# Filler products moved ahead of a gather's transposes, and one routing step fewer ahead of the first expert

## The chip, the cores and the metric

The kernel runs on one core of a Trainium2 chip. The metric is the device time of one execution in microseconds (us): 960.69 before the change, the median of three runs (960.13 to 963.97).

## The reference

Three layers follow each other: a local and global attention, a dense gated layer, and a mixture of 8 experts with balanced routing. The change lies in the last one, which computes this (N = 2304 tokens, D = 512, E = 8 experts, F = 1024):

```python
def _moe2_ref(x, w_gate, w1, w2):
    cap = N // E
    logits = x @ w_gate
    order = np.argsort(-logits.flatten())
    for idx in order:
        tok, e = idx // E, idx % E
        if assigned[tok] >= 0 or counts[e] >= cap:
            continue
        assigned[tok] = e
        counts[e] += 1
    for e in range(E):
        mask = assigned == e
        h = np.maximum(x[mask] @ w1[e], 0.0)
        out[mask] = h @ w2[e]
```

In the kernel there are 17 groups of 128 tokens and each expert takes 272 tokens. The expert that fills first is fixed first, its tokens leave the others' lists, and so on: eight routings, one after the other, each giving the number of an expert and its list of tokens.

## The kernel before, in words

Up to about 652 us the kernel computes attention and the dense layer; the change leaves that alone. Then come eight routings (`route(j)`) and eight experts (`ffn(j)`), and the next routings are woven into the experts.

**A routing.** Each token's best remaining expert is written as a bitmap in bfloat16 (`oh8`, two copies on ScalarE, L929, 2 us together). Then six **counts** search for the threshold, digit by digit: VectorE compares (`ge`, L910 or L948), TensorE counts with 17 products `rt<-ge,oh` (L961), VectorE reads the number and forms the next comparison. After the sixth count the expert's number `ei` is known (L982); SyncE (SP) reads it (L983), and only then can the loads of that expert's weights start. The list of tokens follows: two products with the selected tokens (L1001, L1002), positions on VectorE (L1004 to L1018), 17 products with `obi` (L1022), three with `zs` (L1028), the indices, and three indirect DMAs on GpSimd (POOL) that **gather** the tokens' rows, 128, 128 and 16 of them (`gather`, L1059).

**An expert.** `x_pair(j)` turns the gathered rows with TensorE's transposes (L1101, into the PSUM tile `T`, two buffers) and splits them into a high part `xh` (ScalarE) and a remainder `xl` (VectorE). Weights come as 8 loads of 512 KB (`er`, four buffers, SP, L1071), split the same way: the **cast** `eh` on ScalarE (L1080) and the **remainder** `el` on POOL (L1083). The gate phase makes 8 tiles of 12 products (L1136) in the PSUM tile `A` (three buffers), each read by ScalarE (`fh`) and VectorE (`fl`); the down phase makes 4 tiles of 24 products (L1152). `y_rows(j)` turns the result back (L1115) and scatters it.

**The order.** A scheduler orders each engine's instructions by dependencies and a model; the program narrows this. `visit` notes an instruction of the routing, `behind` orders the next product of an expert after it (and only that one): the routing goes first. `step_route` runs the routing to its next `yield`, and the number yielded says how many parts of the running expert may pass before the next step. `warm(n)` (L879 to L886) makes n **unread products** of 128x512 into an `A` tile, whose result nobody reads; there are three behind each count of routing 0, two behind the first two counts of routing 1, and twenty behind routing 0's last products, in the time in which the first tokens are gathered. At the end of the program's set-up stand `x_pair(0)` and three `step_route()`, then the loop over experts.

Of the kernel before, what the change touches and what calls it, by code (L numbers as in the profile page):

```python
# [24 lines left out]
NT = NTOK // 128  # L25
# [8 lines left out]
def body(ctx, tc, units, gk, gv, wts, w2g, w1, w2, cst, cst2, out):  # L34
    nc = tc.nc
    gp, sy = nc.gpsimd, nc.sync
    NS, SY = (mybir.DependencyInfo(c, mybir.DependencyReason.DATA)
              for c in (mybir.DependencyClass.NoSync, mybir.DependencyClass.Sync))
# [19 lines left out]
    ve, sc, te = nc.vector, nc.scalar, nc.tensor  # L58
# [4 lines left out]
    ident = consts.tile([128, 128], F32, name="ident")  # L63
# [801 lines left out]
    def small(shape, name, dt=F32, bufs=2):  # L865
        return rt.tile(shape, dt, name=name, bufs=bufs)
# [3 lines left out]
    VISIT = []  # L870

    def behind(ins):

        if VISIT:
            tc.add_manual_dep(ins.ins, VISIT.pop().ins.name, NS, reason="routing first")

    def visit(ins):
        VISIT[:] = [ins]

    def warm(n):  # L880

        for _ in range(n):
            pw = p2.tile([128, 512], F32, name="A", bufs=3)
            q = te.matmul(pw, tri, mask.rearrange("p v w -> p (v w)")[:, :512], start=True, stop=True)
            behind(q)
            visit(q)  # L886

    def route(j):

        first = j == 0  # L890
        m = small([128, NT], "m0", bufs=1) if first else M[j % 2]
        S = small([128, 2, NT], "S", BF16)
        if j < NE - 1:
# [3 lines left out]
            oh8 = small([128, NT, 16, NE], "oh8", BF16, bufs=1)  # L897
# [5 lines left out]
            d = small([128, NT], "d0", bufs=1) if first else dplace()  # L903
            lo = small([128, NT], "lo")
            ge = small([128, NT, 64], "ge", BF16, bufs=2)
# [8 lines left out]
            for a, z in ((0, NT - 1), (NT - 1, NT)) if first else ((0, NT),):  # L914
                n = z - a
# [8 lines left out]
                for c0, c1 in cuts:  # L924
# [3 lines left out]
                    else:  # L928
                        q = sc.activation(oh8[:, c0:c1], src, AF.Copy)  # L929
# [11 lines left out]
            for r, th in enumerate((kt0, kt1, kt2, kt3, kt1, kt2)):  # L941
                K = 32 if r % 3 else 64
                if r:
                    ge = small([128, NT, 64], "ge", BF16, bufs=2)
                    for c0, c1 in ((0, 9), (9, NT)):
                        n = c1 - c0
                        tb, db = th[:, None, :].to_broadcast([128, n, K]), d[:, c0:c1, None].to_broadcast([128, n, K])
                        ve.scalar_tensor_tensor(ge[:, c0:c1, :K], tb, nn, db, op0=OP.add, op1=OP.is_le)  # L948
                    e = dplace()
                    ve.tensor_scalar(e, d, nn, 64.0 if r == 3 else 32.0, op0=OP.subtract, op1=OP.mult)  # L950
                    if r % 3 == 2:
                        ve.tensor_scalar(e, e, 1057.0, None, op0=OP.add)
                        if r == 2:
                            ve.tensor_tensor(e, e, lo, op=OP.add)
                    d = e
                if first and r == 0:
                    fill_bank(FIRST_GE[0])
                yield 2 if r == 3 or j == 1 else 3
                pc = p2.tile([128, 512], F32, name="rt", bufs=1)
                for c in range(NT):  # L960
                    visit(te.matmul(pc[:, :K], oh8[:, c].rearrange("p a e -> p (a e)"), ge[:, c, :K],  # L961
                                    start=(c == 0), stop=(c == NT - 1)))
                if j == 0:
                    warm(3)
                elif j == 1 and r < 2:
                    warm(2)
                ok = small([128, 64], "ok", BF16)
                ne = small([128, 1], "ne")
                ve.tensor_scalar(ok[:, :K], pc[:, :K], float(CAP), None, op0=OP.is_ge, op1=OP.add, accum_out=ne)
                nn = small([128, 1], "nn")  # L970
                ve.tensor_reduce(nn, ne.to_broadcast([128, 32]), axis=AX.X, op=OP.max, apply_transpose=True)
# [44 lines left out]
        ve.tensor_tensor(oa, ab[:, 0, :, None].to_broadcast([128, NT, 17]),  # L1016
                         i17[:, None, :].to_broadcast([128, NT, 17]), op=OP.is_equal)
        ve.tensor_tensor(obi, ob, ids_b[:, :, None].to_broadcast([128, NT, 16]), op=OP.mult)  # L1018
        yield 3 if j == 1 else 4
        pz = p2.tile([128, 512], F32, name="rt", bufs=1)  # L1020
        for c in range(NT):
            visit(te.matmul(pz[:17, :16], oa[:, c], obi[:, c], start=(c == 0), stop=(c == NT - 1)))  # L1022
# [5 lines left out]
            visit(te.matmul(pi[:, 16 * g:16 * g + 16], spread[:, g], zs, start=True, stop=True))  # L1028
        if j == 0:
            warm(20)  # L1030
        it = small([128, 3, 16], "it")
        ve.tensor_tensor(it, pi[:, :48].rearrange("p (g b) -> p g b", g=3),
                         pick[:, None, :].to_broadcast([128, 3, 16]), op=OP.mult)
# [59 lines left out]
    def x_pair(j):  # L1093

        xg = XG.pop(j)
        xh = fw.tile([128, 4, CAP], F32R, name="xh", bufs=2)
        xl = fw.tile([128, 4, CAP], F32R, name="xl", bufs=2)
        for g, n in GR:
            pt = p2.tile([128, 4, 128], F32, name="T", bufs=2)
            for d in range(4):  # L1100
                te.transpose(pt[:, d, :n], xg[:n, g, 128 * d:128 * d + 128], ident[:n, :n])  # L1101
            o = slice(128 * g, 128 * g + n)
            XH_LAST[:] = [sc.activation(xh[:, :, o], pt[:, :, :n], AF.Copy)]
            ve.tensor_tensor(xl[:, :, o], pt[:, :, :n], xh[:, :, o], op=OP.subtract)
            if g == 2:
                XP[j] = (xh, xl)
            yield
# [100 lines left out]
    step_route()  # L1208
    for _ in x_pair(0):
        pass  # L1210
    for _ in range(3):
        step_route()
    for j in range(NE):
        while j not in ROUTED:
# [110 lines left out]
```

## Time and profile before

| what | us |
|---|---|
| median of 3 runs | 960.69 (960.13 to 963.97) |
| the profiled execution | 965.33 |
| its span (first to last instruction) | 963.6 |
| TensorE busy, share of the span | 871.9, 90% |
| VectorE | 611.1, 63% |
| ScalarE | 453.0, 47% |
| GpSimd | 371.9, 39% |

The mean granted clock of TensorE is 0.951 of full speed. In the chain of work that ended last TensorE has 68%, VectorE 12%, DMA 5%, and 7% is time in which an engine waited for nothing that the profile shows. Busy shares are means over the whole span: what the routings and the experts wait for is read from windows and timelines of the last third. PE is TensorE, DVE VectorE, ACT ScalarE, POOL GpSimd, SP SyncE.

### The profile page before, as it was taken

The numbers are of one execution on the slowest core, as the hardware profiler recorded it, in microseconds if no ns is written. First come the engines' busy times: TensorE is split into PE (matmuls) and PEld (weight loads), VectorE is DVE, ScalarE is ACT, GpSimd is POOL, SyncE is SP. The second block draws the span as 40 slices with busy tenths as digits, with TensorE's granted clock in tenths as the row PEclk, the third lists the DMA queues.
The fourth block names the chain that finished last, engine by engine and source line by source line (L and its number), as shares of the span: only waits on it lengthen the run. The fifth ranks groups of instructions, "written<-read, shape, count | busy, mean of one in ns | idle before, by whom it ended". The sixth has DMA issues, their size and how long they took to land.

```text
span 963.6 us, 19509 instructions
## 1 busy us (share of the span) xinstructions
PE 871.9 (90%) x7556; PEld 732.3 (76%) x7556; DVE 611.1 (63%) x1859; ACT 453.0 (47%) x923; POOL 371.9 (39%) x344
## 2 busy tenths in 40 slices
PE   5677699999999999989979989996789989999996
PEld 4566578777788887778758757783488988999996
DVE  3677699999328579597595484268666766763210
ACT  4656454555247465445354333230554364545531
POOL 2444333444212222113111111121666786687841
PEclk8889889999999999989989999997789999999998
DMA  9631243542212233303221020001454455446600
GB/s 373 254 121 45 86 155 132 160 161 66 88 66 93 85 103 108 118 29 109 82 78 56 27 74 1 1 23 43 169 184 142 133 185 188 135 149 215 197 28 26
DMA packets 28497, 108.10 MB, mean 112 GB/s; under 512 B 3572, under 2 KB 3572, under 8 KB 28276
## 3 DMA queue, kind: packets, MB, share of 16 engines
q1 hardware_dynamic: 25332, 97.94, 30.0%
q0 software_dynamic: 3072, 8.92, 2.6%
q8 instruction: 59, 0.97, 0.4%
q14 instruction: 34, 0.28, 0.1%
HBM read 97.92 MB, written 8.91 MB: 111 GB/s over the span
## 4 chain that ended last, share of the span: by engine, by line
PE 68%; DVE 12%; issue 7%; DMA 5%; POOL 4%; ACT 3%; SPq 0%; POOLq 0%; ACTq 0%; DVEq 0%
PE G L564 26%; PE X L588 11%; PE A L1152 7%; PE A L1136 5%; PE rt L961 2%; DMA er<-w 2%; DMA xg<-xs,idx 2%; DVE junk L523 2%; DVE ge L948 1%; POOL wp L50 1%; PE PV L476 1%; PE PV L399 1%; POOL vl L50 1%; PE T L1101 1%; DMA gkr<-gv 1%
## 5 line engine op out<-in xcount | busy, mean ns | idle before, releaser
L564 PEld LDWEIGHTS <-wp 128*128 128x128 f16 x2592 | 231.6, 99 | 80.5 <-issue 52.0
L564 PE MATMUL G<-xth,wp 128*128 128x256 f16 (+1 forms) x1344 | 235.8, 270 | 4.1 <-ACT xth L434 2.5
L578 POOL TENSOR_TENSOR hl<-th,hh 128x256 fp32r<-128x256 f32 (+1 forms) x108 | 85.5, 792 | 348.1 <-ACT hh L576 274.8
L564 PE MATMUL G<-xtl,wp 128*128 128x256 f16 (+1 forms) x672 | 177.5, 270 | 4.3 <-DVE xtl L435 4.3
L1083 POOL TENSOR_TENSOR el<-er,eh 128x1024 fp32r<-128x1024 f32 x62 | 146.3, 2390 | 40.7 <-ACT eh L1080 40.4
L569 ACT ACTIVATE th<-G,ib 128x256 f32<-128x256 f32 (+1 forms) x108 | 49.4, 459 | 107.8 <-PE G L564 97.0
L571 DVE SCALAR_TENSOR_TENSOR th<-th,G 128x256 f32<-128x256 f32 (+1 forms) x108 | 43.4, 402 | 81.9 <-ACT th L569 81.0
L1080 ACT ACTIVATE eh<-er 128x1024 fp32r<-128x1024 f32 x64 | 65.5, 1054 | 49.4 <-DMA er<-w 43.2
L576 ACT ACTIVATE hh<-th 128x256 fp32r<-128x256 f32 (+1 forms) x108 | 43.4, 402 | 75.4 <-DVE th L573 75.1
L1136 PE MATMUL A<-xh,eh 128*128 128x272 f32 x256 | 77.9, 304 | 0.0
L1152 PE MATMUL A<-fh,eh 128*128 128x272 f32 x256 | 76.6, 302 | 0.0
L1136 PE MATMUL A<-xh,el 128*128 128x272 f32 x256 | 75.2, 294 | 0.0
L1136 PE MATMUL A<-xl,eh 128*128 128x272 f32 x256 | 74.9, 293 | 0.0
L1152 PE MATMUL A<-fh,el 128*128 128x272 f32 x256 | 74.4, 292 | 0.0
L1152 PE MATMUL A<-fl,eh 128*128 128x272 f32 x256 | 74.2, 291 | 0.0
L1141 DVE SCALAR_TENSOR_TENSOR fl<-A,fh 128x272 fp32r<-128x272 f32 x64 | 28.0, 439 | 59.2 <-ACT fh L1140 57.4
L523 DVE SCALAR_TENSOR_TENSOR junk<-xr,w2gt 128x512 f16<-128x512 f32 x80 | 59.0, 737 | 4.1 <-ACT xr L500 3.4
L588 PE MATMUL X<-oh,hh 128*128 128x512 f32 x156 | 57.7, 444 | 2.1 <-ACT hh L576 2.1
L588 PE MATMUL X<-oh,hl 128*128 128x512 f32 x156 | 55.7, 428 | 0.0
L573 DVE SCALAR_TENSOR_TENSOR th<-th,ib,G 128x256 f32<-128x256 f32 (+1 forms) x108 | 50.1, 464 | 2.9
L588 PE MATMUL X<-ol,hh 128*128 128x512 f32 x156 | 51.5, 403 | 0.0
L1136 PEld LDWEIGHTS A<-xl,eh 128*128 128x128 f32 x256 | 49.2, 192 | 0.1
(389 smaller groups left out, 2126.7 us busy)
## 6 DMA issues: line engine op xcount, KB each, us to landing
er<-w SPq DMA_DIRECT2D x64, 512.0 KB, 5.2
wr<-wts SPq DMA_DIRECT2D x36, 512.0 KB, 3.6
unit<-units SPq DMA_DIRECT2D x22, 688.0 KB, 4.0
unit<-gv SPq DMA_DIRECT2D x12, 640.0 KB, 3.8
wp<-units SPq DMA_DIRECT2D x10, 688.0 KB, 7.8
gkr<-gk SPq DMA_DIRECT2D x8, 608.0 KB, 4.7
xs<-xr SPq DMA_DIRECT2D x17, 256.0 KB, 2.0
gkr<-gv SPq DMA_DIRECT2D x4, 640.0 KB, 7.3
```

The lines of the kernel that those rows point to most:

```text
L523: ve.scalar_tensor_tensor(junk[:, :DM], xr, 1.0, w2gt[:, e], op0=OP.mult, op1=OP.mult, accum_out=L[:, c, e:e + 1])
L564: te.matmul(pg[:, j, :n], wp_[:, f, j, a, o], x[:, d, :n], start=(i == 0), stop=(i == 11))
L569: TH[:] = [sc.activation(th[:, :n], pg[:, 0, :n], AF.Tanh, scale=ib[:, 0, f:f + 1])]
L571: ve.scalar_tensor_tensor(t[:, :n], th[:, :n], 1.0, pg[:, 0, :n], op0=OP.add, op1=OP.mult)
L573: mark(ve.scalar_tensor_tensor(h[:, :n], t[:, :n], ib[:, 1, f:f + 1], pg[:, 1, :n], op0=OP.mult, op1=OP.mult))
L576: sc.activation(hh[:, :n], h[:, :n], AF.Copy)
L578: gp.tensor_tensor(hl[:, :n], h[:, :n], hh[:, :n], op=OP.subtract)
L588: te.matmul(self.px[t], a[:, 128 * t:128 * t + 128], w[:, f, :], start=(f == 0 and i == 0), stop=(f == NF - 1 and i == 2))
L1080: q = sc.activation(h, r, AF.Copy)
L1083: q = (ve if j == 0 and i < 2 else gp).tensor_tensor(l, r, h, op=OP.subtract)
L1136: behind(te.matmul(pa_[:, :CAP], a[:, s], x[:, d], start=(i == 0), stop=(i == 11)))
L1152: behind(te.matmul(py[:, :CAP], a[:, s], x[:, f], start=(i == 0), stop=(i == 23)))
```

## The change

Four edits, all in the last layer:

1. The first transpose of `x_pair(0)` is ordered behind the last of the twenty unread products.
2. The first product of routing 1's first count is ordered behind the last transpose of `x_pair(0)`.
3. Two steps instead of three of the next routing in front of the first expert.
4. From routing 2 on the first count comes 5 parts after the step before instead of 3, and the products with `obi` of routing 1 come 4 parts after instead of 3.

```diff
+    WARM, T_LAST = [], []
+
     def visit(ins):
         VISIT[:] = [ins]
+        return ins
...
-                yield 2 if r == 3 or j == 1 else 3
+                yield 2 if r == 3 or j == 1 else 5 if r == 0 and j > 1 else 3
                 pc = p2.tile([128, 512], F32, name="rt", bufs=1)
                 for c in range(NT):
-                    visit(te.matmul(pc[:, :K], oh8[:, c].rearrange("p a e -> p (a e)"), ge[:, c, :K],
-                                    start=(c == 0), stop=(c == NT - 1)))
+                    q = visit(te.matmul(pc[:, :K], oh8[:, c].rearrange("p a e -> p (a e)"), ge[:, c, :K],
+                                          start=(c == 0), stop=(c == NT - 1)))
+                    if j == 1 and r == c == 0:
+                        tc.add_manual_dep(q.ins, T_LAST[0].ins.name, NS, reason="tokens first")
...
-        yield 3 if j == 1 else 4
+        yield 4
         pz = p2.tile([128, 512], F32, name="rt", bufs=1)
...
             warm(20)
+            WARM[:] = VISIT
...
-                te.transpose(pt[:, d, :n], xg[:n, g, 128 * d:128 * d + 128], ident[:n, :n])
+                q = te.transpose(pt[:, d, :n], xg[:n, g, 128 * d:128 * d + 128], ident[:n, :n])
+                T_LAST[:] = [q]
+                if WARM:
+                    tc.add_manual_dep(q.ins, WARM.pop().ins.name, NS, reason="behind the unread products")
...
     for _ in x_pair(0):
         pass
-    for _ in range(3):
+    for _ in range(2):
         step_route()
```

The line numbers of the changed kernel are 3 higher from L879 on and 6 to 9 higher after L1028. All products are the same in number and kind; what moves is their order. Three places show it.

TensorE, between the last of routing 0 and the first count of routing 1, before (`cb` and `mask` are operands of the unread products, `T<-ident,xg` the transposes, `rt<-ge,oh` the count):

```order
L884 MATMUL A<-mask,cb 128x512
L1101 MATMUL T<-ident,xg 128x128 x4
L884 LDWEIGHTS cb
L884 MATMUL A<-mask,cb 128x512
...
L884 MATMUL A<-mask,cb 128x512
L1101 MATMUL T<-ident,xg 128x128 x4
L884 LDWEIGHTS cb
L884 MATMUL A<-mask,cb 128x512
L961 LDWEIGHTS oh_8643
L961 MATMUL rt<-ge,oh_8643 128x64
```

and changed:

```order
L887 LDWEIGHTS cb
L887 MATMUL A<-mask,cb 128x512
L1107 MATMUL T<-ident,xg 128x128 x8
L1107 MATMUL T<-ident,xg 128x16 x4
L964 LDWEIGHTS oh_8643
L964 MATMUL rt<-ge,oh_8643 128x64
```

Before, ten unread products stand in front of the first four transposes, nine behind them, one behind the next four, and the third group of transposes stands behind the first count. Now twenty stand in front of all twelve transposes and the count behind them.

ScalarE, in the second expert, before (`eh` casts of the third expert's weights, `oh` the two bitmap copies of routing 3, `fh` gate tiles, `yo` result rows):

```order
L1140 ACTIVATE fh<-A 128x272 x2
L1116 ACTIVATE yo<-Y 128x512
L1080 ACTIVATE eh<-er 128x1024
L1140 ACTIVATE fh<-A 128x272 x2
L1080 ACTIVATE eh<-er 128x1024
L1116 ACTIVATE yo<-Y 128x512
L1080 ACTIVATE eh<-er 128x1024
L1140 ACTIVATE fh<-A 128x272
L1080 ACTIVATE eh<-er 128x1024
L929 ACTIVATE oh_9649<-oh_9648 128x1152
L929 ACTIVATE oh_9649<-oh_9648 128x1024
```

and changed:

```order
L1149 ACTIVATE fh<-A 128x272 x4
L1125 ACTIVATE yo<-Y 16x512
L1086 ACTIVATE eh<-er 128x1024
L1149 ACTIVATE fh<-A 128x272 x2
L1086 ACTIVATE eh<-er 128x1024 x4
L932 ACTIVATE oh_9695<-oh_9694 128x1152
L932 ACTIVATE oh_9695<-oh_9694 128x1024
```

The copies stood behind the fourth cast of these weights and stand now behind the fifth; four gate tiles instead of two are read in front of the first cast.

POOL, around the gather of the third expert's tokens, before (`el` remainders, `xg` gathers, `out` scatters):

```order
L1083 TENSOR_TENSOR el<-er,eh 128x1024 x9
L1059 DMA xg<-xs,idx 128x512 x2
L1059 DMA xg<-xs,idx 16x512
L1083 TENSOR_TENSOR el<-er,eh 128x1024 x5
L1118 DMA out<-yo,idx 2176x512
L1083 TENSOR_TENSOR el<-er,eh 128x1024 x2
L1118 DMA out<-yo,idx 2176x512
L1083 TENSOR_TENSOR el<-er,eh 128x1024
L1059 DMA xg<-xs,idx 128x512 x2
L1059 DMA xg<-xs,idx 16x512
```

and changed:

```order
L1089 TENSOR_TENSOR el<-er,eh 128x1024 x10
L1065 DMA xg<-xs,idx 128x512 x2
L1065 DMA xg<-xs,idx 16x512
L1089 TENSOR_TENSOR el<-er,eh 128x1024 x4
L1127 DMA out<-yo,idx 2176x512 x3
L1089 TENSOR_TENSOR el<-er,eh 128x1024 x5
L1065 DMA xg<-xs,idx 128x512 x2
L1065 DMA xg<-xs,idx 16x512
```

The second pair of `xg` rows is the third expert's gather. Before, 17 remainders had been made since the first gather when it comes; now 19. The three scatters of the first expert's rows stood apart and now follow each other.

## Rows read from the trace of the kernel before

**Rows 1.** Windows over the experts: length, busy of each engine (instructions), clock, DMA.

```profile
693.00:953.90 260.90, 247.96 (x2430) 239.91 (x2429) 137.17 (x529) 121.09 (x205) 179.34 (x102) 0.98 0.44 144
825.00:953.00 128.00, 127.09 (x1151) 124.54 (x1150) 46.90 (x173) 58.15 (x103) 86.01 (x49) 1.00 0.40 130
```

**Rows 2.** Windows by stage, first gather to second expert, same columns.

```profile
674.50:677.50 3.00, 3.00 (x8) 1.07 (x9) 2.46 (x7) 2.31 (x3) 1.36 (x1) 0.50 1.02 412
677.50:682.70 5.20, 0.84 (x4) 0.21 (x2) 3.59 (x11) 3.53 (x4) 4.58 (x4) 0.83 0.84 295
682.70:687.70 5.00, 4.99 (x15) 2.53 (x16) 0.69 (x1) 0.99 (x2) 2.54 (x2) 0.50 0.32 89
687.80:708.20 20.40, 16.46 (x215) 14.82 (x214) 16.41 (x68) 8.49 (x14) 9.99 (x5) 1.00 0.34 120
708.30:715.00 6.70, 6.70 (x30) 6.42 (x29) 3.83 (x17) 4.80 (x7) 6.55 (x4) 0.50 0.60 194
715.10:745.50 30.40, 28.94 (x319) 27.88 (x318) 19.12 (x77) 13.74 (x23) 20.64 (x12) 1.00 0.48 154
...
749.30:752.50 3.20, 3.20 (x30) 3.08 (x30) 1.28 (x5) 1.94 (x3) 2.57 (x4) 0.50 0.88 287
```

**Rows 3.** Timeline of TensorE, first expert: start, us, instruction [idle before <-releaser].

```profile
690.70 0.74 PE L961 MATMUL rt<-ge,oh 128*128 128x32 bf16 x17 [0.99 <-DVE ge L948]
...
693.12 0.37 PE L1136 MATMUL A<-xh,eh 128*128 128x272 f32 x1
...
706.66 0.59 PE L1022 MATMUL rt<-obi,oa 128*17 128x16 f32 x17 [2.11 <-DVE b L1040]
...
719.35 0.74 PE L961 MATMUL rt<-ge,oh 128*128 128x32 bf16 x17 [0.99 <-DVE ge L948]
```

**Rows 4.** Timeline, start of the second expert, ScalarE and TensorE.

```profile
731.55 0.58 PE L961 MATMUL rt<-ge,oh 128*128 128x32 bf16 x17
...
738.78 1.06 ACT L1080 ACTIVATE eh<-er 128x1024 fp32r<-128x1024 f32 x1 [2.62 <-DMA er<-w]
...
741.43 0.50 PE L1028 MATMUL rt<-zs,spread 17*128 17x16 f32 x3 [0.45 <-DVE zs L1024]
...
745.72 2.10 ACT L929 ACTIVATE oh<-oh 128x1152 bf16<-128x1152 bf16 x2
...
747.52 0.90 PE L961 MATMUL rt<-ge,oh 128*128 128x64 bf16 x17 [1.95 <-DVE ge L910]
```

**Rows 5.** Timeline of the front, TensorE and GpSimd.

```profile
674.56 3.78 PE L884 MATMUL A<-mask,cb 128*128 128x512 bf16 x10
...
678.43 0.96 POOL L1059 DMA_INDIRECT xg<-xs,idx  x1 [0.30 <-issue]
...
682.71 1.12 PE L1101 MATMUL T<-ident,xg 128*128 128x128 f32 x4 [4.37 <-DMA xg<-xs,idx]
...
683.62 4.05 PE L884 MATMUL A<-mask,cb 128*128 128x512 bf16 x9
...
687.46 0.76 PE L1101 MATMUL T<-ident,xg 128*128 128x128 f32 x4
...
688.27 0.66 PE L961 MATMUL rt<-ge,oh 128*128 128x64 bf16 x17
```

**Rows 6.** Chain of waits, front and first two experts: start, us, what.

```profile
676.14 6.52 DMA xg<-xs,idx
...
697.73 1.60 PE A L1136 x12
...
735.26 8.18 DMA er<-w
```

**Rows 7.** The page: one group of part 5, one line of part 6.

```profile
L1083 POOL TENSOR_TENSOR el<-er,eh 128x1024 fp32r<-128x1024 f32 x62 | 146.3, 2390 | 40.7 <-ACT eh L1080 40.4
...
er<-w SPq DMA_DIRECT2D x64, 512.0 KB, 5.2
```

**Rows 8.** Timeline of TensorE, transposes for the fourth expert.

```profile
785.60 1.35 PE L1101 MATMUL T<-ident,xg 128*128 128x128 f32 x8 [0.84 <-DMA xg<-xs,idx]
```

## The prediction

> **What bounds the kernel now.** I read the share of busy time first: TensorE is busy for 90% of the span, but that is a mean over stages, so I went on to windows over the last third, the only part that the change touches. From the first product of the first expert to the last one TensorE is busy 247.96 of 260.90 us, and from 825 us on 127.09 of 128.00 [rows 1]. So after 825 nothing is to be had, and between 693 and 825 at most 12.9 us of idle time. The second loss is the clock. In four stretches the granted clock is 0.50, that is 1.2 instead of 2.4 GHz [rows 2]. Two of them lie inside the experts, 6.7 and 3.2 us long. What ran there at half speed would have taken half as long, so they cost 3.4 + 1.6 = 5.0 us. In front of each TensorE had waited: 2.11 us before the product at 706.66 [rows 3] and 1.95 us before the one at 747.52 [rows 4]. The waits of 0.99 us at 690.70 and 719.35 [rows 3] left the clock at 1.00 [rows 2].
>
> The third place is the front, 674.5 to 693.1: the gather of the first expert's tokens, its transposes, the first counts of routing 1. The timeline of that stretch [rows 5] shows ten unread products, 4.37 us of idle time on the gather, four transposes, nine more unread products of 4.05 us, and only then the second group of transposes. The chain of waits [rows 6] gives the gather 6.52 us from its start at 676.14.
>
> **The change, part by part.** The profiled execution took 965.33 us, 4.64 above the median of 960.69; I take the differences against it and carry them to the median.
>
> *Unread products in front.* All twenty now lie inside the wait. Ten took 3.78 us, mostly at half clock, and nine took 4.05 [rows 5], so one costs 0.43 at half clock and half of that, 0.21, at full. From 674.56 seven run at half speed until 677.5, where the clock rises [rows 2], and thirteen follow in 2.8 us: done at about 680.3, before the transposes can start at 682.71. If the clock stayed low, twenty would take 8.5 us and end at 683.06, 0.35 late. Either way the extra ten are covered by the gather. What they gave back is in the other place: the second group's transposes need no longer wait for nine products until 687.46. They wait for the second gather instead: it starts at 678.43 [rows 5] and, at the 6.52 us of the first, lands near 685.0 (an estimate from these two rows). Transposes of 0.76 us and the small third group bring routing 1's first count from 688.27 to about 686.4. The further counts keep their pace; with one step fewer ahead of the expert, its third count comes behind the first twelve products of the expert. The first product moves from 693.12 to about 689.75. By the end of the sixth count 48 instead of 36 products are done, and the count itself is 1.0 us earlier. Twelve products take 1.60 us [rows 6], so the lead is **2.6 us**. Between ends: 3.4 (the whole move of the first product) and 0.
>
> Against it stands the clock. The nine products that filled 683.6 to 687.7 are gone; TensorE is now patchy from 680 to 690 (a wait of some 2.4 us on the first gather, shorter ones behind it). The 4.37 us of waiting was followed by clock 0.50 until 687.7 [rows 2]. If that low stretch now reaches into the first expert by the length of the shortest seen, 3.2 us, it costs 1.6. I take half of it, 0.8, so this part gives **-1.8**, with ends -3.4 and 0.
>
> *First expert, routing 1's last steps.* The 2.11 us in front of the product at 706.66 [rows 3] came from VectorE's chain of positions, which begins with the sums over the selected tokens. The yields put more products behind those sums, but the down phase now in front of it needs the last gate tiles, read by ScalarE and VectorE, and VectorE now takes one of these in front of the positions. A wait of about 1 us on the tile and one of about 1.2 on the positions replace one of 2.11. I take **0** for wait and clock; the ends are 0 and -5.5 (the wait and the 3.4 of clock both gone).
>
> *Routing 2's second count.* With five parts instead of three after the first bitmaps, products cover the 0.99 us at 719.35 [rows 3]: **-1.0**. Routing 2 however ends later against the experts: its sixth count stood at 731.55, in front of all products of the second expert; now it stands behind some thirty of that expert's products, 4.0 us of work at 1.60 for twelve [rows 6].
>
> *Second expert: routing 3 behind the weights.* The sixth count of routing 2 gives the number of the next expert, and its weights are loaded from then on. Routing 3's bitmap copies lie on ScalarE behind casts of these weights: four before (the copies at 745.72, the first count at 747.52, which waited 1.95 us) [rows 4], five now. One cast is 1.06 us [rows 4]. The fifth needs a buffer that a cast and GpSimd's remainder free first, and its load, so the copies come 1.1 us later or more; a load takes 5.2 us in the middle and 8.18 with four in flight [rows 6, 7], so 3 us more is the other end. What covers this is shorter now. Behind the sixth count stand 48 products and some transposes, 7.0 us, then the last gate tile: its buffer is free once ScalarE and VectorE have read another tile behind the first cast, which starts 7.2 us after that count (738.78) and takes 1.06, with 0.8 for the two readers: 9.1, a wait of 2.0. Then 36 products and two short steps, 6.0 us, so TensorE comes to the first count of routing 3 at 15.1 to 15.7 and finds it free at 16.3 + 1.1 = 17.4: a wait of 1.6 to 2.3. With 1.3 for small ones (today's 0.45 at routing 2's last step among them) that is 5.3, where 0.45 and 1.95 stand today, 2.4: **+2.9**, ends 0 and +6.
>
> *Third and fourth expert.* Their gathers move behind one or two more remainders on GpSimd, 2.39 us each [rows 7]; the transposes at 785.60 wait 0.84 us on one now [rows 8]. On the other side every wait in the second expert lets routing catch up, and from 825 on hardly a wait is left. **-1.2** for these two, ends -3 and +5. For one more stretch at half clock I add **+0.6**, from the 1.6 that a short one costs. From the fifth expert on nothing changes, and one load's place on SP's queue is hidden behind the weights already in the buffers: 0, at most the 0.9 us that are idle from 825 on.
>
> Sum: -1.8 + 0 - 1.0 + 2.9 - 1.2 + 0.6 = **-0.5 us**: 964.8 for a profiled execution, **960.2** at the median. About 0.5%, 4.8 us, is what a measurement of this kernel can tell from no change.
>
> **The rivals.**
> *The clock holds* (faster). If the new waits in the first two experts stay near 1 us each, like the two that left the clock at 1.00, the low stretches of 3.4 and 1.6 us vanish, and so do the 0.8 and 0.6 that I added: -0.5 - 6.4 = -6.9, or 953.8; if only the first one goes, 956.8; I say 955. For it: the wait of 2.11 is split in two. Against it: the two halves lie within a few us of each other, and no row shows two such waits close together that left the clock up. The Trainium skill, page "TensorE: Matmul & The Clock Gate", section "Why this matters for your kernels", warns only of longer gaps between bursts than these; by it the clock would hold through all of them and this rival would be the forecast. The trace disagrees: waits of 2.11 and 1.95 us were followed by clock 0.50.
>
> *The routing becomes the bound* (slower). Copies of routings 3, 4 and 5 one cast later, 1.06 each, the fifth load landing after 8.2 instead of 5.2 us, and the third expert's gather behind two remainders of 2.39: 3.2 + 3.0 + 4.8 = 11 at most; with a third hidden, some 7 more than forecast, **967**. It decides once routing 3's first count ends over 17.5 us after routing 2's sixth (748.42 - 732.13 = 16.3 now, 17.4 forecast). For it: the fourth expert waits on its tokens already. Against it: the experts' products fill much of it, and after 825 routing has caught up.
>
> *The twenty do not fit.* If the clock stays low, the transposes come 0.35 us late: 960.5, and the change gains nothing in the gather's wait.
>
> **How the numbers follow.** Forecast, waits exchanged for waits: 0.43. The twenty that do not fit: 0.07, same side. Clock holds: 0.26. Routing the bound: 0.24. Under 955.9 lies the fast rival, over 965.5 the slow one: faster 0.26, same 0.50, slower 0.24. The range leaves out about one in ten on each side: 953.5 is the fast rival at its full size, 968 the slow one with 8 us. The forecast's own range is 956 to 965.
>
> **What would show it.** Right: no unread product after the first transposes, and the second group's near 685; first expert product near 689.8; no wait at routing 2's second count; in the second expert a wait of 1.5 us or more on routing 3's first count, with the bitmap copies behind the fifth cast; clock 0.50 once in the first and once in the second expert. Wrong: no stretch at half clock after 690 (fast), or transposes of the third and fourth expert that wait over 2 us on their gathers (slow), or a low clock that lasts well into the first expert.

## The result and the profile after

The change takes **973.51 us** (median of 7 runs, 968.02 to 974.41), the kernel before 962.89 (7 runs, 957.69 to 964.50). The ratio is 1.0106, 95% interval 1.0078 to 1.0134: slower by 10.6 us, outside the forecast range of 953.5 to 968. The page of the change:

```profile
span 972.4 us, 19507 instructions
...
PE 877.1 (90%) x7556; PEld 734.8 (76%) x7556; DVE 613.9 (63%) x1859; ACT 453.9 (47%) x923; POOL 371.9 (38%) x344
```

Its profiled execution took 974.20 us, span 972.4 against 963.6 before. TensorE's share of busy time is 90% in both, which tells nothing; the windows do.

The front came out as forecast. TensorE, from the last of routing 0 to the first product of the first expert (answers to [rows 5]):

```profile
672.01 6.15 PE L887 MATMUL A<-mask,cb 128*128 128x512 bf16 x20
680.43 0.66 PE L1107 MATMUL T<-ident,xg 128*128 128x128 f32 x4 [2.27 <-DMA xg<-xs,idx]
682.59 1.65 PE L1107 MATMUL T<-ident,xg 128*128 128x128 f32 x8 [1.50 <-DMA xg<-xs,idx]
684.17 1.09 PE L964 MATMUL rt<-ge,oh 128*128 128x64 bf16 x17
...
687.43 0.79 PE L1145 MATMUL A<-xh,eh 128*128 128x272 f32 x1
```

All twenty unread products run ahead of the transposes, in 6.15 us; the second group follows the first after 1.50 us on its gather, and no filler stands between. From the first unread product to the first product of the first expert 15.42 us pass, against 18.56 before (693.12 - 674.56): 3.1 us are gained. The clock is low until 689.1:

```profile
687.40:689.10 1.70, 1.70 (x8) 1.61 (x7) 1.55 (x6) 1.49 (x2) 1.70 (x2) 0.51 0.01 5
747.10:753.90 6.80, 6.29 (x34) 6.17 (x34) 2.38 (x8) 3.05 (x5) 6.02 (x6) 0.50 0.66 203
764.20:767.50 3.30, 3.30 (x31) 3.18 (x30) 1.00 (x3) 0.38 (x1) 0.00 (x0) 0.50 0.00 0
798.30:801.70 3.40, 3.40 (x23) 3.06 (x21) 2.82 (x7) 0.60 (x1) 3.40 (x2) 0.50 0.00 0
852.90:856.30 3.40, 3.40 (x18) 3.40 (x16) 2.09 (x8) 1.85 (x3) 3.20 (x3) 0.50 0.44 106
```

The first row is the part that reaches into the first expert: 1.7 us, cost 0.85. The other four lie in the second expert (two of them), the third and the fifth; together they are 16.9 us at half clock where before had 9.9 [rows 2].

Where the time went shows in windows cut at the first product of each expert (length first; then busy time of PE, PEld, DVE, ACT, POOL; then the clock). Before, first to sixth expert, then the last two:

```profile
693.10:732.00 38.90, 35.62 (x390) 34.27 (x386) 27.27 (x108) 16.91 (x26) 28.84 (x15) 0.91 0.37 124
732.00:767.70 35.70, 33.22 (x348) 32.17 (x344) 24.04 (x97) 16.72 (x28) 24.61 (x14) 0.95 0.48 151
767.70:803.70 36.00, 32.99 (x360) 31.43 (x357) 24.62 (x100) 17.33 (x29) 24.64 (x14) 1.00 0.55 180
803.70:837.80 34.10, 30.88 (x335) 29.39 (x332) 23.13 (x91) 16.85 (x29) 24.59 (x14) 1.00 0.53 179
837.80:872.80 35.00, 34.09 (x357) 32.74 (x356) 22.22 (x92) 18.43 (x31) 26.56 (x16) 1.00 0.49 163
872.80:901.60 28.80, 28.80 (x247) 28.34 (x245) 8.49 (x24) 15.84 (x28) 26.42 (x16) 1.00 0.58 182
901.60:953.90 52.30, 52.27 (x417) 51.47 (x415) 7.30 (x17) 18.92 (x38) 23.59 (x14) 1.00 0.21 73
```

After, the whole stretch ahead of the same seven:

```profile
687.40:962.40 275.00, 255.01 (x2441) 244.23 (x2439) 140.47 (x532) 122.53 (x206) 179.29 (x102) 0.97 0.42 137
687.40:724.70 37.30, 34.08 (x369) 32.03 (x367) 26.30 (x102) 17.38 (x27) 26.57 (x14) 0.98 0.39 129
724.70:767.40 42.70, 37.41 (x357) 35.38 (x357) 23.34 (x90) 17.33 (x28) 26.99 (x16) 0.88 0.38 125
767.40:802.40 35.00, 30.83 (x295) 28.96 (x290) 20.44 (x79) 16.65 (x27) 24.25 (x14) 0.95 0.48 153
802.40:840.30 37.90, 35.62 (x386) 33.54 (x387) 25.78 (x101) 17.62 (x29) 24.10 (x15) 1.00 0.43 142
840.30:873.80 33.50, 29.98 (x310) 28.82 (x308) 20.17 (x78) 16.59 (x27) 23.06 (x15) 0.95 0.50 159
873.80:909.70 35.90, 34.43 (x321) 33.42 (x318) 15.86 (x67) 16.44 (x28) 25.62 (x16) 1.00 0.57 180
909.70:962.40 52.70, 52.66 (x423) 52.07 (x421) 8.58 (x19) 20.52 (x41) 28.69 (x17) 1.00 0.28 92
```

The first expert is 1.6 us shorter, the second 7.0 longer. From there on the first products of an expert run among the last of the one before, so I read the next four in pairs: the third and fourth together are 2.8 us longer, the fifth and sixth 5.6, the rest 0.4. With the 3.1 gained in the front that is a loss of 11.1 us. (The spans differ by 8.8 only because this execution reached the front 2.55 us earlier, 672.01 against 674.56.) Over the experts the idle time of TensorE is 275.00 - 255.01 = 20.0 us, 12.9 before [rows 1]. The busy time is 7.1 us longer for the same expert products; the low clock, 18.6 us with the 1.7 above, explains about (18.6 - 9.9) / 2 = 4.35 of that, the rest I did not take apart.

What TensorE waits for in these experts, from the list of waits (us in total, times, longest), and two places in the timeline; the first line is the longest row on ScalarE before:

```profile
PE Y L1115 <- ACT yo L1116: 1.4, 2, 0.7
...
PE Y L1124 <- ACT yo L1125: 4.9, 3, 3.2
PE A L1145 <- DVE fl L1150: 3.0, 3, 1.5
PE rt L964 <- ACT oh L932: 2.4, 2, 1.9
...
PE T L1107 <- DMA xg<-xs,idx: 1.8, 2, 1.2
```

```profile
736.98 1.06 ACT L1086 ACTIVATE eh<-er 128x1024 fp32r<-128x1024 f32 x1 [2.25 <-DMA er<-w]
...
737.94 0.67 ACT L1149 ACTIVATE fh<-A 128x272 fp32r<-128x272 f32 x2
...
738.85 0.39 PE L1145 MATMUL A<-xh,eh 128*128 128x272 f32 x1 [1.48 <-DVE fl L1150]
...
745.48 2.09 ACT L932 ACTIVATE oh<-oh 128x1152 bf16<-128x1152 bf16 x2
...
746.68 0.43 PE L964 MATMUL rt<-ge,oh 128*128 128x64 bf16 x9 [1.88 <-ACT oh L932]
...
850.06 1.06 ACT L1086 ACTIVATE eh<-er 128x1024 fp32r<-128x1024 f32 x1 [3.86 <-DMA er<-w]
...
851.30 0.59 ACT L1125 ACTIVATE yo<-Y 128x512 f32<-128x512 f32 x1
...
851.94 0.60 PE L1124 MATMUL Y<-ident,yt 128*16 128x128 f32 x4 [3.23 <-ACT yo L1125]
```

In the second expert ScalarE stands 2.25 us at the first cast `eh` of the next weights, because the load has not landed; two gate tiles behind it are read late, and TensorE waits 1.48 us for a free tile. The bitmap copies behind more casts hold the first count of routing 3 up for another 1.88. In the fifth expert ScalarE stands 3.86 us at such a cast; the result row `yo` behind it is read at 851.30, and TensorE waits 3.23 us with the next transposes. The list of waits of before has no row of more than 1.4 us on ScalarE.

### The profile page after: what moved, and what is told of

Same layout as the page of the kernel before. It is cut to its first block, busy times and chain, and to the rows that moved or that the text cites. A ratio compares the mean times of both kernels' runs of the same rounds, so it can differ in the third digit from the quotient of the medians.

```text
span 972.4 us, 19507 instructions
## 1 busy us (share of the span) xinstructions
PE 877.1 (90%) x7556; PEld 734.8 (76%) x7556; DVE 613.9 (63%) x1859; ACT 453.9 (47%) x923; POOL 371.9 (38%) x344
## 4 chain that ended last, share of the span: by engine, by line
PE 63%; DVE 12%; DMA 8%; issue 7%; POOL 5%; ACT 4%; SPq 1%; POOLq 0%; ACTq 0%
PE G L564 26%; PE X L588 10%; PE A L1161 6%; PE A L1145 5%; DMA er<-w 5%; DMA xg<-xs,idx 2%; DVE junk L523 2%; PE rt L964 2%; POOL el L1089 1%; PE PV L476 1%; POOL wp L50 1%; POOL vl L50 1%; PE PV L399 1%; DMA gkr<-gv 1%; DVE ge L951 1%
## 5 line engine op out<-in xcount | busy, mean ns | idle before, releaser
L1161 PE MATMUL A<-fh,eh 128*128 128x272 f32 x256 | 78.8, 310 | 0.6 <-DVE fl L1150 0.6
L1145 PEld LDWEIGHTS A<-xh,eh 128*128 128x128 f32 x256 | 49.3, 193 | 4.8 <-DVE fl L1150 3.8
```

What stands on the lines that cost most here:

```text
L1145: behind(te.matmul(pa_[:, :CAP], a[:, s], x[:, d], start=(i == 0), stop=(i == 11)))
L1161: behind(te.matmul(py[:, :CAP], a[:, s], x[:, f], start=(i == 0), stop=(i == 23)))
```

## Experiments

Each kernel ran beside the one before on the same chip; medians of before lay between 960.9 and 966.8, so I compare ratios (those on record, which can differ by 0.2% from the quotients of the medians). The expectations are in us for a before of 962.9 and are read by ratio too. Only before ran in all five rounds (e1 to e4, e5 to e8, e9 to e12, e13 to e15, e16 to e18); kernels of different rounds are compared through it alone. Two counts are read from the order of instructions: where the **sixth count** of routings 2 to 6 stands, in products behind the start of the second to sixth expert (negative: ahead of it), and how many **gate tiles are cut**, that is, have at least four products of other tiles between their own twelve (second to seventh expert).

| kernel | sixth counts | cut | ratio (95%) |
|---|---|---|---|
| before | 0, -24, -48, -75, -72 | 9 | 1 |
| e1 front alone | 0, -24, -48, -75, -72 | 9 | 0.9982 (0.9962 to 1.0002) |
| **the change** | 30, 28, 18, 5, -12 | 23 | 1.0106 (1.0078 to 1.0134) |
| e2 without the 5 parts | 28, 5, -19, -41, -65 | 21 | 1.0140 (1.0113 to 1.0167) |
| e3 three steps | 28, 18, 5, -12, -19 | 18 | 1.0081 (1.0055 to 1.0107) |
| e4 list after 3 parts | 24, 12, 0, 0, -24 | 2 | 0.9948 (0.9930 to 0.9965) |
| e9 list after 5 parts | 36, 24, 12, 0, 0 | 4 | 1.0005 (0.9984 to 1.0026) |
| e10 list after 2 parts | 28, 18, 5, -12, -19 | 18 | 1.0092 (1.0058 to 1.0126) |
| e8 front, two steps | 12, 0, -24, -48, -72 | 9 | 1.0068 (1.0045 to 1.0090) |
| e11 front, list after 4 | 18, -12, -36, -60, -72 | 20 | 0.9996 (0.9975 to 1.0018) |
| e12 front, 5 parts | 12, 0, 0, -24, -24 | 5 | 1.0000 (0.9976 to 1.0024) |
| e5 change, fixed loads | 30, 18, 18, 5, -12 | 22 | 0.9975 (0.9956 to 0.9994) |
| e6 before, fixed loads | 0, -24, -48, -75, -72 | 8 | 0.9956 (0.9935 to 0.9977) |
| e7 change, late casts | 42, 28, 18, 5, -12 | 23 | 1.0104 (1.0079 to 1.0130) |
| e13 as e4, rows later | 24, 12, 0, 0, -24 | 3 | 1.0006 (0.9986 to 1.0026) |
| e14 change, rows later | 30, 28, 18, 5, -12 | 23 | 1.0100 (1.0062 to 1.0137) |
| e15 as e4, four tiles | 24, 12, 0, 0, -24 | 6 | 1.0033 (1.0013 to 1.0052) |
| **e16 change, tiles kept whole** | 36, 24, 12, 5, -6 | 3 | 0.9940 (0.9918 to 0.9962) |
| e17 as e10, tiles kept whole | 24, 12, 5, -6, -19 | 3 | 0.9990 (0.9972 to 1.0008) |
| e18 as e4, all tiles whole | 24, 12, 0, 0, -24 | 0 | 1.0023 (1.0000 to 1.0046) |

### Which edit costs: e1 to e4

e1 leaves only the two orderings of the front:

```diff
-    for _ in range(2):
+    for _ in range(3):
...
-                yield 2 if r == 3 or j == 1 else 5 if r == 0 and j > 1 else 3
+                yield 2 if r == 3 or j == 1 else 3
...
-        yield 4
+        yield 3 if j == 1 else 4
```

e2 undoes the second of these alone, e3 the first, e4 the third.

> Only the two orderings of the front are left (twenty unread products in front of the transposes, first count behind the last transpose); three steps and the old yields are back, and from the first expert on the order of TensorE is nearly that of before. Theory A, late routing (the sixth count of each routing falls into the next expert's gate phase, the first cast then waits for its load on ScalarE among gate tiles, and TensorE waits for what is queued behind it): those waits are gone, and the first product comes some 2 us earlier: 958 to 962 where before is 962.9 and the change 973.5. Theory B, the front (a lower clock around the transposes reaches into the experts): slower than before by 5 us or more. Theory C (bitmap copies one cast later): like A.

> The change with 3 parts instead of 5 in front of the first count of routing 2 and later. Sixth counts stand 28, 5, -19, -41 products behind the start of the second, third, fourth, fifth expert, where the change has 30, 28, 18, 5 and before 0, -24, -48, -75. The bitmap copies still stand behind the fifth cast for routing 3. Theory A: the second expert loses as with the change, the later ones do not: 5 to 8 us of the 10.6 come back, 966 to 968. Theory C (copies behind the fifth cast): under 3 us come back. Theory B: nothing comes back.

> The change with three steps in front of the first expert as before; yields as changed. Sixth counts stand 28, 18, 5, -12 products behind the starts of the second to fifth expert. Theory A: a part of the loss comes back, 2 to 5 us: 968 to 972. Theory D (the two steps alone cost the time, since the first expert starts with routing 1 one step behind): all comes back, 962.

> The change with 3 parts instead of 4 in front of the list steps of routing 1. Sixth counts stand 24, 12, 0, 0 products behind the starts of the second to fifth expert. Theory A: 3 to 6 us come back: 967 to 971. Theories B, C and D: nothing comes back, except that under C the copies of routing 3 stand behind the fourth cast again, which is worth 1 to 3 us.

Measured: e1 963.04 us where before took 966.23, e2 977.93, e3 973.37, e4 960.70. The front is not the loss: theory B falls. So does theory A as I had put it (the later the sixth count, the slower): e2 moves the counts ahead and is no faster than the change, and e4 is faster than theory A allowed. Theory C priced the place of the copies at 1 to 3 us, far less than e4 gives back, so it does not carry the loss alone; whether it has a part is taken up behind e16. One yield of one part, 4 instead of 3 ahead of routing 1's list products, separates 1.0106 from 0.9948, with all else as in the change. Theory D gets 0.25% back, within the intervals.

### Is it the cast that waits for its load: e5 to e7, and two steps: e8

In e5 (the change) and e6 (before) the weights come from a fixed index, so these two leave out choosing each expert's own weights; in e7 the first cast of each set is issued later and ordered behind the last read of a tile or row:

```diff
-        q = sy.dma_start(r, src[bass.ds(EV[j], 1), :, c:c + 1024].rearrange("e p c -> (e p) c"))
+        q = sy.dma_start(r, src[j:j + 1, :, c:c + 1024].rearrange("e p c -> (e p) c"))
```

```diff
+            READ[:] = [sc.activation(hh[:, f], pa_[:, :CAP], AF.Relu)]
...
+        if i == 0 and READ:
+            tc.add_manual_dep(q.ins, READ[0].ins.name, NS, reason="read tiles first")
...
-        if SQ and SQ[0] in when and now - when[SQ[0]] >= 4:
+        if SQ and SQ[0] in when and now - when[SQ[0]] >= (10 if SQ[0][1] == 0 else 4):
```

e8 is e1 with two steps.

> The change with every expert's weights loaded from a fixed index: the loads no longer wait for the number that the routing finds (the tokens meet the wrong expert's weights; sizes and all other work are the same). Sixth counts keep their late places: 30, 18, 18, 5, -12 products behind the experts' starts. Theory A2, head of the queue (the first cast of a set of weights waits on ScalarE for its load, gate tiles, result rows and bitmap copies stand behind it, TensorE waits for these, and the clock falls): those waits go, 8 to 13 us come back, 961 to 966. Theory E, late routing costs by itself (lists and gathers later, products cut into more pieces): at most 3 us come back, 970 or more.

> The same fixed loads in the kernel before, as the yardstick for the last run. In its trace only 0.45 us of waits stand near a first cast, so by theory A2 at most 4 us are gained, and the distance between change and before shrinks from 10.6 to under 4 us. By theory E the distance stays near 10.

> The change with the first cast of each set of weights issued six parts later and ordered behind the gate tile or result row read last; the loads are as in the change. Theory A2: the waits on gate tiles and result rows behind the first casts (1.48, 1.38, 3.23, 1.47 us) vanish, while the bitmap copies come up to 3 us later: 965 to 971. Theory E: no faster than the change, 973 or more.

> The front orderings and two steps ahead of the first expert, with all yields of before. Sixth counts 12, 0, -24, -48, -72 products behind the starts of the second to sixth expert; result rows stand behind the third and fourth set's first cast. Theory A2: one or two waits of about 1.5 us there, no more: 960 to 966. Theory D (two steps alone cost the time): over 970.

Measured: e5 958.64, e6 956.39 (before: 960.85). The change falls from 1.0106 to 0.9975, before only to 0.9956: of the distance of 1.06% there remain 0.19%. The two rows of waits that were 4.9 and 3.0 us in the change are in e5:

```profile
PE Y L1124 <- ACT yo L1125: 0.7, 1, 0.7
...
PE A L1145 <- DVE fl L1150: 0.5, 3, 0.2
```

So a first cast that stands blocked among the gate tiles is needed for the loss. e5 takes away both halves of that at once: its first casts of the third to sixth set start 30, 24, 47 and 17 products before the running expert begins. e7 missed: 969.51, and by ratio, 1.0104, it gains nothing. The waits at the first casts went, but ScalarE now stands at a later cast of the same set, and TensorE waits behind it again, 1.41 us on a tile in the third expert (two lines) and 1.96 in the fifth. The transposes also wait 7.3 us on gathers where the change waits 1.8. Where they wait, the gathers are not later: the third expert's is issued after 117 products of the second, in the change after 121, but its transposes stand after 123 instead of 168:

```profile
780.38 1.06 ACT L1086 ACTIVATE eh<-er 128x1024 fp32r<-128x1024 f32 x1 [2.10 <-DMA er<-w]
...
782.25 0.39 PE L1164 MATMUL A<-fh,eh 128*128 128x272 f32 x1 [1.41 <-DVE fl L1153]
...
PE T L1110 <- DMA xg<-xs,idx: 7.3, 7, 2.5
```

e8 missed as well, 966.63, ratio 1.0068, above the 966 that I gave as the upper end. It has few cut tiles; its time goes to counts that wait for the bitmap copies, and to gathers:

```profile
PE rt L964 <- ACT oh L932: 5.6, 7, 1.6
PE T L1107 <- DMA xg<-xs,idx: 4.9, 5, 2.3
```

With the 5 parts (e4) the same row is 1.2 us in all. Two steps and 5 parts belong together.

### Late or in the middle of a tile: e9 to e12

e9 and e10 change one number of the change:

```diff
-        yield 4
+        yield 5 if j == 1 else 4
```

(2 in e10.) e11 is e1 with the 4 parts for the list, e12 is e1 with the 5 parts for the first counts.

> The change with 5 parts instead of 4 in front of routing 1's list products: one part, half a tile of the gate phase, later still. The sixth counts move to 36, 24, 12, 0, 0 products behind the starts of the second to sixth expert: whole tiles of 12 again, as with 3 parts (24, 12, 0, 0, -24), where the change has 30, 28, 18, 5, -12. Theory F, the half tile (a step of the routing that falls into the middle of a gate tile leaves half a tile less of work in front of the buffer that the blocked ScalarE must free): fast, 957 to 965. Theory G, lateness (the later the sixth count, the more stands behind the first cast): as slow as the change or slower, 973 to 978.

> The change with 2 parts in front of routing 1's list products: sixth counts at 28, 18, 5, -12, -19, earlier than with 3 parts in the later experts or nearly equal, but in the middle of tiles. Theory F: slow, 970 to 976. Theory G: between, 962 to 967.

> The front orderings and the 4 parts in front of routing 1's list products alone; three steps, 3 parts in front of the first counts. Sixth counts at 18, -12, -36, -60: one half tile in the second expert, whole tiles after it. Theory F: one wait of about 1.5 us and its clock, 963 to 968. Theory G: earlier than in the change throughout, little lost: 961 to 965.

> The front orderings and the 5 parts in front of the first counts; three steps and 3 parts for the list. Sixth counts at 12, 0, 0, -24, -24: whole tiles, and the first counts come late enough for the bitmap copies. Theories F and G: fast, 955 to 961.

Measured: e9 962.14, e10 969.48, e11 960.33, e12 960.60 (before: 961.67). One part later is fast again, and one part earlier than e4 is slow: with 2, 3, 4, 5 parts the ratio is 1.0092, 0.9948, 1.0106, 1.0005. A part of the gate phase is half a tile, six products. Lateness (G) falls as the whole cause; what counts is whether the routing's steps stand between tiles or inside them. e11 shows that cut tiles alone do no harm (20 of them, ratio 0.9996): there the first casts of the third to sixth set start after 64, 33, 17 and -9 products of the running expert, in the change after 77, 70, 65 and 48. The same part more ahead of the list, 4 instead of 3, costs 0.14% from e1 to e11, 0.7% from e8 to e2, 0.8% from e12 to e3 and 1.6% from e4 to the change, each with some 0.3 to 0.4% of uncertainty: it costs most where the first casts come latest. By ratio e12 comes out 2 us above its range, e11 inside G's and just under F's.

### What a half tile does: e13 to e18

e13 shifts the transposes of result rows by one part in e4, e14 by two parts in the change; e15 gives e4 four tile buffers (in all three places that make an `A` tile):

```diff
-            if part == 1 and now % 4 == 0:
+            if part == 1 and now % 4 == 1:
```

```diff
-            pa_ = p2.tile([128, 512], F32, name="A", bufs=3)
+            pa_ = p2.tile([128, 512], F32, name="A", bufs=4)
...
-            pt = p2.tile([128, 4, 128], F32, name="T", bufs=2)
+            pt = p2.tile([128, 4, 128], F32, name="T", bufs=1)
```

> The version with 3 parts for the list (sixth counts on whole tiles: 24, 12, 0, 0, -24), with the transposes of result rows one part later than in the change. Their reads on ScalarE now stand behind the first cast of the third to fifth set of weights instead of in front, as they do in the change; sixth counts and gate tiles keep their places. Theory F1, the rows (the half tile costs because a row read falls behind the blocked cast and the next row's transposes wait for the only buffer): waits of 1.3 to 3 us on result rows at those casts, 965 to 971. Theory F2, the gate tiles and the cut tiles themselves: stays at 957 to 963.

> The change with the transposes of result rows two parts later: sixth counts as in the change (30, 28, 18, 5, -12), the row read in front of the third set's first cast instead of behind it, the other sets as in the change. Theory F1: the wait near the third set (1.38 us and its share of the clock) changes, the 3.23 and 1.47 us at the fifth and sixth stay: 970 to 974. Theory F2: 972 to 976, nothing changes.

> The version with 3 parts for the list, with four buffers instead of three for product tiles and one instead of two for the token transposes. Sixth counts unchanged. If tiles behind the first casts are what is left there (2.5 us of waits on tiles in its trace), 1 to 3 us are gained, 957 to 960; if the single transpose buffer costs more, up to 3 us are lost.

Measured: e13 962.31, e14 970.11, e15 964.69 (before: 961.36). With the row reads behind the casts and the tiles whole (e13) only 0.3 us of waits stand on rows near the casts; the rows are not the cause, though e13 lies 0.6% above e4. e14 stays as slow as the change, which fits both theories; but the wait that F1 said would change, 1.38 us, is 1.69 us and is on a gate tile. The fourth buffer in exchange for a transpose buffer does not pay, and the change itself was not run with four.

The order of TensorE shows what else differs. In the second expert, gate tiles f4 to f7 with the number of their products:

```
the change: f4 6, f5 9, sums, f5 2, sums, f4 6, f5 1, f6 6, f7 6, (down) 18, list, f6 6, zs, f7 6
e4:         sums, f4 12, f5 12, list, f6 12, zs, f7 12, (down)
```

`behind` orders the next product of the expert behind the routing's last one. If the step falls into a tile, that next product is the tile's seventh: the tile is already open, holds one of three buffers, and is finished only after the routing's product, while other tiles overtake it. In the change f4 is read behind the blocked cast, and the product that waits 1.48 us at 738.85 is the first of f7, which needs f4's buffer. In the fifth expert of the change six products lie between the second and the third group of row transposes, in e16 twelve and the list's 17; there the wait is the 3.23 us on the row's read. e16 lets `behind` act on the first product of a tile alone; e17 does so in e10, e18 in e4, there in the down phase too:

```diff
-                    behind(te.matmul(pa_[:, :CAP], a[:, s], x[:, d], start=(i == 0), stop=(i == 11)))
+                    q = te.matmul(pa_[:, :CAP], a[:, s], x[:, d], start=(i == 0), stop=(i == 11))
+                    if i == 0:
+                        behind(q)
```

> The change with one edit: in the gate phase only the first product of a tile is ordered behind the routing's last product, not whichever product comes next. A tile that has begun is then finished: in the second expert f3 to f7 run 12 products each, where the change has 6 of f4, 11 of f5, 6 of f4, 6 of f6, 6 of f7 and so on. Sixth counts move later: 36, 24, 12, 5, -6. Theory H, cut tiles (a tile cut by the routing's step stays open behind it and holds one of three buffers while others overtake, so the blocked ScalarE stops TensorE a tile earlier): the loss goes, 958 to 965, the waits on tiles near the first casts and half of the time at half clock with it. Theory G (lateness): 973 or more. Theory F1 (rows): no change, 970 or more.

> The version with 2 parts for the list (969.5, ratio 1.0092) with the same edit; its second expert then runs tiles of 12, sixth counts 24, 12, 5, -6, -19. Theory H: 958 to 964. Theories G and F1: 967 to 971.

> The fastest version so far (3 parts for the list, sixth counts 24, 12, 0, 0, -24), with the edit in gate and down phase. Its gate tiles are whole already; only the down tiles, which it cuts too, change. Theory H: 0 to 3 us faster than before's 0.9948, as tiles stay whole in the down phase; if the routing's counts come too late for that, up to 4 us slower.

Measured: e16 **960.84**, e17 964.95, e18 969.19 (before: 966.83). The change falls from 1.0106 to 0.9940, e10 from 1.0092 to 0.9990, although e16's routing is about as late as the change's: its sixth counts move both ways, and its first casts start after 82, 72, 58 and 48 products, against 77, 70, 65 and 48. (In e10 and e4, slow and fast, they start after 69, 63, 47, 35 and 71, 60, 47, 37.) Its second expert, and its waits:

```profile
739.33 1.06 ACT L1086 ACTIVATE eh<-er 128x1024 fp32r<-128x1024 f32 x1 [2.03 <-DMA er<-w]
...
740.29 0.38 ACT L1151 ACTIVATE fh<-A 128x272 fp32r<-128x272 f32 x1
...
741.55 0.38 ACT L1151 ACTIVATE fh<-A 128x272 fp32r<-128x272 f32 x1
...
746.70 0.42 PE L964 MATMUL rt<-ge,oh 128*128 128x64 bf16 x9 [0.45 <-DVE ge L913]
```

```profile
PE rt L964 <- ACT oh L932: 1.1, 3, 0.5
...
PE Y L1124 <- ACT yo L1125: 0.7, 1, 0.7
PE A L1145 <- DVE fl L1152: 0.5, 1, 0.5
```

The first cast still waits 2.03 us for its load. Behind it the next tile is read as in the change, but no product waits for a tile there; the three rows on result rows, tiles and copies that made up 10.3 us in the list above are 2.3. The mean clock over its experts is 0.99, where the change has 0.97:

```profile
690.00:948.50 258.50, 247.19 (x2431) 237.31 (x2428) 140.34 (x534) 122.20 (x205) 179.68 (x102) 0.99 0.45 146
```

What stays open is the share of the bitmap copies (theory C). In the change, e2, e3, e10 and e14, all slow, routing 3's copies stand behind the fifth cast, in e4, e9, e16 and e17 behind the fourth (in e5, with fixed loads and fast, behind the sixth), and no run moves them alone. So of the 7.0 us lost in the second expert, the 1.88 us on the copies and the half clock behind them may be theirs. They cannot be the whole: from the fifth expert on the copies stand behind the fourth cast in the change as well. And e11 and e7, with cut tiles and the copies behind the fourth cast, are the one fast and the other slow.

e18, the control, missed on the wrong side: 0.75% above e4. It waits 7.3 us on gathers, like e7. The gathers of the third to fifth expert are issued after 120, 114 and 96 products, in e4 after 123, 114 and 103, so they are not later there; the third expert's transposes stand after 144 products instead of 156. What whole down tiles change beyond that was not tried. e16 beats both kernels, and e4 does as well; the two were not run beside each other.

## Why the prediction was wrong

**The front: right.** Twenty products fit, the second transposes come behind their gather, and the first product gained 3.1 us (forecast 3.4, with 0.8 lost to the low clock; measured 0.85). The 0.8 was half of a guess, so that it fits is luck.

**The first expert, term 0: on the good side.** The wait ahead of the list products is 0.68 us instead of 2.11, and no low clock follows. Two waits of the row transposes on ScalarE's reads, 0.85 and 1.27 us, take back 2.1; the expert is 1.6 us shorter.

**Routing 2's second count: right,** its 0.99 us are gone.

**The second expert, +2.9 and +0.6 for the clock: place and waits right, price too small.** Forecast were about 2.0 us on a gate tile and 1.6 to 2.3 on routing 3's first count, with the copies behind the fifth cast; measured 1.48 and 1.88, and the copies stand there. But two stretches at half clock, 6.8 and 3.3 us, followed, which cost 5.0 us where 1.6 before and the 0.6 that I added make 2.2; the expert lost 7.0 instead of 3.5.

**The step that failed** is this one: "every wait in the second expert lets routing catch up" and "From the fifth expert on nothing changes: ... 0, at most the 0.9 us". From the fifth expert on the change loses 5.6 + 0.4 = 6.0 us, more than half of the result, where the forecast has 0; the waits of 3.23 and 1.47 us on result rows and the 1.7 of the stretch at half clock lie there. The third and fourth expert, forecast to gain 1.2, lose 2.8. Two things were missed. First, the yields of one routing add up to 30 parts now (28 before) of the 32 of an expert, so routing gains two parts per expert on the experts instead of four; the order shows it, sixth counts 30, 28, 18, 5 against 0, -24, -48, -75. The first casts therefore stay among gate tiles up to the sixth expert, where before they had moved ahead of them by the fourth. Second, I read the cut tiles in the order (six products of one, nine of the next) as a list of products to be counted, and did not ask what an open tile holds. e16 shows that the orderings inside tiles are the cause: keep the begun tiles whole, and the loss of 1.06% turns into a gain of 0.6%, with routing about as late. e5 shows the other condition: a cast among the gate tiles that has to wait for its load. That the open tile acts through its buffer is read from order and timeline and was not tested with more buffers, and the copies' share in the second expert is open.

**The rivals.** "Routing becomes the bound" had the direction and the kind of place (casts, copies, a load that lands late), and its point of decision, 17.5 us from routing 2's sixth count to routing 3's first, was crossed: from 730.56 to 748.68, 18.1. But what was to show it, transposes of the third and fourth expert that wait over 2 us on their gathers, did not come (1.8 us in two waits); its mechanism was lateness alone, which e9 and e16 rule out, as late and fast; and its price of 967, some 7 us over the forecast, ended with the fourth expert. "The clock holds" was right for the first expert alone. The Trainium skill's section that I set against the trace ("TensorE: Matmul & The Clock Gate", "Why this matters for your kernels") would have no low clock behind waits like these; three of the four low stretches follow waits of 0.8 to 1.9 us, the fourth one of 3.23.

## What to carry to other kernels

When an ordering edge says "the next product goes behind this", look at where in an accumulation it lands: on a tile's first product it delays work that holds nothing, inside a tile it leaves a buffer open, and the loss shows up far away, where another engine stands at an instruction that has to wait (here ScalarE at a cast). A yield count sets where in a tile a step falls as well as how late it comes; try its neighbours on both sides before believing that later is worse. And when a lead changes, work out from the counts whether the loop regains it per round; a slip that is not regained can be paid in every round.

## What the runs showed of the hardware

I had not expected the same wait to act on the clock so differently. The 2.11 us ahead of the first expert's list products, which before was followed by clock 0.50 [rows 2, 3], left it at 1.00 in e4 (the product is L1027 there):

```profile
704.94 0.59 PE L1027 MATMUL rt<-obi,oa 128*17 128x16 f32 x17 [2.11 <-DVE b L1046]
...
708.50:715.00 6.50, 6.50 (x67) 6.44 (x66) 3.81 (x15) 4.52 (x6) 6.05 (x4) 1.00 0.65 187
```

In e9 the wait was 3.09 us, and the clock fell:

```profile
709.10 0.66 PE L1027 MATMUL rt<-obi,oa 128*17 128x16 f32 x17 [3.09 <-DVE b L1046]
...
708.50:715.00 6.50, 5.90 (x40) 5.68 (x40) 5.51 (x23) 3.22 (x4) 6.50 (x4) 0.50 0.58 182
```

The same 2.11 us stand in front of this product in e1, e8, e12, e13 and e15 too: the clock stayed at 1.00 behind it in the first four and fell to 0.50 from 706.4 to 713.3 in e15. So a single wait of 2 us can cost nothing more, or the 3.4 us of a low stretch of 6.7; what decides between them these runs do not show, and a forecast has to carry both.
